# The joined score step of a fused attention and SwiGLU kernel: query groups stored one behind the other, and its exponential issued in two parts

## The chip, the cores and the metric

The kernel runs on one core of one Trainium2 chip. The metric is the device time of one execution in microseconds, smaller is better. The engines are named as in the profile: PE (matrix unit; PEld its weight loads), DVE (vector), ACT (scalar, with the exponentials), POOL (GpSimd) and SP (which here only issues DMAs).

## The reference

The attention has 8 batches of 8 heads, 576 positions and 64 values per head. Its result goes, row by row, through an RMS norm and a SwiGLU block.

```python
scores = scale * np.matmul(q, k.transpose(0, 1, 3, 2))          # B=8 H=8 S=576 D=64
cum = np.cumsum(np.maximum(s, 0.0), axis=-1)
bias = -(cum[:, :, :, None] - cum[:, :, None, :])
scores = np.where(causal, -1000000000.0, scores + np.minimum(bias, 0.0))
attn = softmax(scores)                                          # written out in the original
attn_out = np.matmul(attn, v)
x = attn_out.transpose(0, 2, 1, 3).reshape(B * S, H * D)        # 4608 x 512
xn = x / np.sqrt(np.mean(x * x, -1, keepdims=True) + 1e-6) * rms_g
g = xn @ w_gate                                                 # 512 -> 1536
out = (g * sigmoid(g) * (xn @ w_val)) @ w_out                   # 1536 -> 512
```

## The kernel before, in words

**The outer loop.** The 4608 tokens are worked off in nine chunks of 512 by `ffn(c)`. A chunk has twelve blocks of a gate product (L946) and a value product (L955), each of four matmuls into a bank `psF`; ACT takes the tanh (L949), DVE forms `U` (L958) and `Ht` (L951). Then `store` makes four output tiles of twelve matmuls each (L972), which ACT copies to `osb` (L976). Four `psF` banks are shared by all of these.

**What is threaded through it.** Between groups of matmuls `ffn` calls `step()`, a hand-written planner that counts slots. It puts a score step, a piece of attention-times-values (`av_step`, L437 and L443), a transpose or a DMA issue into the stream when its tables say that its inputs are due. The attention of batch b+1 and later is so computed beside the matmuls of earlier chunks. Each engine runs its instructions in the order in which they were written.

**How keys and queries lie.** For batches 3 to 7 (`MB = 3`), transposed keys and queries come from DMA transposes (L190, issued on SP) into `kqT`. The view `kqTx[d, parity, w, c, h, n]` has the chunk c of 128 positions, the pair of heads h, and position n. For queries (w = 1) of chunks 0 to 3 the 128 positions lie in the order (r p): position 4p + r stands at 32r + p. The 64 positions of the tail, chunk 4, lie in natural order. The two heads of a pair are on partitions 0 to 63 and 64 to 127, so that one matmul of 64 rows is issued for each (`par` 0 and 1).

**The score step.** `s_run(b, kb)` does one key chunk `kb` for all eight heads of such a batch. It takes four banks: one `psF`, one `psT`, and the two halves of `psS`; a bank holds two heads of 256 columns each (`j * 256`). For kb = 0, 1, 2 a head's 256 columns are the queries of chunks kb and kb+1. For kb = 3, the joined step (`join`), they are the 128 queries of chunk 3 against key chunk 3, the 64 tail queries against key chunk 3, and the 64 tail queries against key chunk 4. There is one joined step in each of the batches 3 to 7, five in all. In the kernel before, the three groups are interleaved in the bank: for each r the bank holds 32 columns of the first group, 16 of the second and 16 of the third. The tail is read with a step of four positions to fit.

**After the scores.** `exp_q` holds the four exponentials, one for each bank, and `step()` issues one per slot on ACT. Each one reads the bank with the (r p) order turned and writes `E` in natural order (bf16). After the second of a pair, POOL zeroes what lies above the diagonal (`mask`, L384): two selects in a joined step, one otherwise. `av_step` reads `E` as weights on PE some slots later.

Of the kernel before, what the change touches and what calls it, by code (L numbers as in the profile page):

```python
# [12 lines left out]
AF = mybir.ActivationFunctionType  # L13
# [13 lines left out]
def kernel(  # L27
# [12 lines left out]
    nc = tc.nc  # L40
# [41 lines left out]
    kqTx = kqT.rearrange("d a w (c h n) -> d a w c h n", c=NSC, h=HP)  # L82
# [26 lines left out]
    def psF():  # L109
        return pp.tile([128, DM], FP32, name="psF", tag="F", bufs=4)  # L110
# [4 lines left out]
    def psS():  # L115
        return pp.tile([128, 2, 512], FP32, name="psS", tag="S", bufs=1)
# [10 lines left out]
    def psT32():  # L127
        return pp.tile([128, 512], FP32, name="psT32", tag="T", bufs=1)
# [114 lines left out]
    def take_slot(key, reads):  # L243
        sl = ecount[0] % NE
        ecount[0] += 1
        eslot[key] = sl
        eread[sl] = reads
        return sl
# [90 lines left out]
    def s_run(b, kb):  # L339


        p, join = b % 2, kb == 3
        N = 192 if join else 256
        fb, tt, ps = psF(), psT32(), psS()
        banks = {1: (fb, tt), 0: (ps[:, 0, :], ps[:, 1, :])}
        es = {g: take_slot((b, kb, g), 3 if join else 2) for g in (1, 0)}
        if join:
            eslot.update({(b, 4, g): es[g] for g in es})

        def keys(rs, c, hp):  # L350
            return kqTx[rs, p, 0, c, hp, :] if b >= KB else kqTn[rs, p, 0, hp, c * 128:c * 128 + 128]

        for g in (1, 0):
            for j in (0, 1):
                hp = 2 * g + j
                parts = [(kb, kqTx[:, p, 1, kb:kb + 2, hp, :], 0, 256)]
                if join:
                    tail = kqTx[:, p, 1, 4, hp, 0:64].rearrange("d (p r) -> d r p", r=4)
                    parts = [(3, kqTx[:, p, 1, 3, hp, :].rearrange("d (r p) -> d r p", r=4), 0, 32),
                             (3, tail, 32, 16), (4, tail, 48, 16)]  # L360
                for i, (c, qT, o, n) in enumerate(parts):
                    for par in (0, 1):
                        rs = slice(par * 64, par * 64 + 64)
                        to = banks[g][par][:, j * 256:j * 256 + 256]
                        if join:
                            to = to.rearrange("k (r p) -> k r p", r=4)[:, :, o:o + n]
                        nc.tensor.matmul(to, lhsT=keys(rs, c, hp), rhs=qT[rs],  # L367
                                         start=(j == 0 and i == 0), stop=(j == 1 and i == len(parts) - 1))


        def exps(g, par):
            to = E[:, es[g], 2 * par:2 * par + 2, :]
            src = banks[g][par]
            if join:
                to = to.rearrange("k j (p r) -> k j p r", r=4)
                src = src.rearrange("k (j r p) -> k j p r", j=2, r=4)
            else:
                to = to.rearrange("k j (a p r) -> k (j a) p r", a=2, r=4)
                src = src.rearrange("k (j r p) -> k j p r", j=4, r=4)
            nc.scalar.activation(out=to, in_=src, func=AF.Exp, scale=0.125)  # L380

        def mask(g, c, q0, nq):
            Ev = E[:, es[g], :, q0:q0 + nq]
            nc.gpsimd.affine_select(  # L384
                out=Ev, in_=Ev, pattern=[[0, 4], [1, nq]], compare_op=ALU.is_ge, fill=0.0, base=0,
                channel_multiplier=-1)
            done["S", b, c, g] = slot[0]

        def part(g, par):
            exps(g, par)  # L390
            if g:
                last[("RA", "RT")[par]] = slot[0]
            if par:
                after(MLAG, lambda: mask(g, kb, 0, 128))
                if join:
                    after(MLAG, lambda: mask(g, 4, 192, 64))

        last["RA"] = last["RT"] = 10 ** 6
        exp_q.extend((join, lambda a=(g, par): part(*a)) for g in (1, 0) for par in (0, 1))
# [145 lines left out]
    def after(n, f):  # L545
        delayed.append((slot[0] + n, f))
# [158 lines left out]
    def do_s(key, pair=None, masked=False):  # L705
        b, kb, g = key
        last["S"] = done["R", b, kb] = slot[0]
        if b >= MB:
            last["run"] = done["R", b, 4] = slot[0]
            return s_run(b, kb)  # L710
        second = s_step(b, kb, g, pair, masked)
        done["S", b, kb, g] = slot[0]
        if kb == 4:
            done["S", b, 4, 1] = slot[0]
        return second
# [350 lines left out]
    with tc.manual_schedule():  # L1066
# [7 lines left out]
        for w in (0, 1):  # L1074
# [8 lines left out]
            out=mneg.rearrange("p (j n) -> p j n", j=2), in_=mneg.rearrange("p (j n) -> p j n", j=2),  # L1083
# [361 lines left out]
```

## Time and profile before

| | us |
|---|---|
| median of three runs (355.47 to 356.57) | 355.63 |
| the profiled execution | 355.58 |
| its span, first to last instruction | 354.1 |
| PE busy in the span | 340.6 (96%) |
| DVE, ACT, POOL busy | 276.9, 213.4, 204.5 |
| PE's granted clock, mean | 0.999 |

The profiled execution is 1.5 us longer than its span and 0.05 us below the median. A row of the timeline gives a start, a duration, the engine, the source line and what it writes and reads; where equal instructions follow each other they are one row with a count, whose duration runs from the first start to the last end. Matmuls overlap: their durations hold the way through the array, so that the distance of two starts, not the duration, says how long PE was taken.

### The profile page before, as it was taken

The page shows a single profiled execution, that of the slowest core. Times are in us where ns is not written, and L with a number is a line of the kernel's source. Part 1 is how long each engine was busy: PE and PEld are TensorE (multiplying, and loading weights), DVE is VectorE, ACT ScalarE, POOL GpSimd, SP SyncE. Part 2 cuts the span into 40 slices and gives each one's busy share as a digit, 9 for nine tenths or more (in the row PEclk, how much of TensorE's full clock was granted, in tenths as well). Part 3 has the DMA queues.
Part 4 walks back from the last instruction along what each step waited for, and adds up shares of the span by engine and source line. Part 5 has one row for each costly group of instructions (what it writes and reads, how often), then busy time and mean ns, then how long its engine had stood idle before and what let it go on. Part 6 is the DMA issues. An engine that isn't in the chain of part 4 may idle for free.

```text
span 354.1 us, 6889 instructions
## 1 busy us (share of the span) xinstructions
PE 340.6 (96%) x2374; PEld 165.3 (47%) x2419; DVE 276.9 (78%) x524; ACT 213.4 (60%) x471; POOL 204.5 (58%) x337
## 2 busy tenths in 40 slices
PE   5989999999999999999999999999999999999995
PEld 2445444544444444444554454444544554444443
DVE  6697989598967887798889887988798659836840
ACT  3988885878786546855677557654565445224321
POOL 6969754456769986687597987597745310000000
PEclk9999999999999999999999999999999999999999
DMA  7999999999969998999899999495510121020002
GB/s 220 142 213 270 180 175 259 181 211 181 98 123 177 146 179 118 233 141 202 143 170 105 117 131 185 46 113 90 143 29 17 57 94 23 0 91 30 0 34 93
DMA packets 130528, 45.68 MB, mean 129 GB/s; under 512 B 110548, under 2 KB 125656, under 8 KB 130488
## 3 DMA queue, kind: packets, MB, share of 16 engines
q0 software_dynamic: 67056, 13.70, 50.5%
q1 hardware_dynamic: 53792, 24.20, 33.3%
q10 hardware_dynamic: 9640, 7.29, 8.2%
q8 instruction: 20, 0.33, 0.4%
q14 instruction: 20, 0.16, 0.2%
HBM read 37.90 MB, written 9.44 MB: 134 GB/s over the span
## 4 chain that ended last, share of the span: by engine, by line
PE 77%; DVE 8%; POOL 4%; issue 4%; DMA 3%; ACT 2%; SPq 0%; DVEq 0%; POOLq 0%; ACTq 0%
PE psF L972 25%; PE psF L955 21%; PE psF L946 20%; DVE U L958 2%; PE psAV L443 2%; DMA kq<-in_q_dram 2%; DMA kqT<-kqn 2%; PE psS L286 2%; DVE Ht L951 1%; PE psAV L437 1%; DVE x_sb L453 1%; PE psF L367 1%; POOL v_sb L409 1%; POOL v_sb L194 1%; PE psS L367 1%
## 5 line engine op out<-in xcount | busy, mean ns | idle before, releaser
L955 PE MATMUL psF<-xnT,wv_sb 128*128 128x512 bf16 x424 | 109.9, 379 | 0.4
L946 PE MATMUL psF<-xnT,wg_sb 128*128 128x512 bf16 x414 | 109.0, 379 | 1.3 <-ACT xnT L511 0.3
L949 ACT ACTIVATE T<-psF 128x512 f32<-128x512 f32 x108 | 64.6, 598 | 62.9 <-PE psF L946 58.8
L972 PE MATMUL psF<-wout_sb,Ht 128*128 128x512 bf16 (+2 forms) x428 | 98.9, 373 | 1.4 <-issue 0.8
L958 DVE SCALAR_TENSOR_TENSOR U<-T,psF 128x512 bf16<-128x512 f32 x108 | 73.7, 682 | 24.1 <-ACT T L949 23.9
L951 DVE TENSOR_TENSOR Ht<-U,psF 128x512 bf16<-128x512 bf16 x99 | 67.8, 685 | 6.9
L972 PEld LDWEIGHTS <-Ht 128*128 128x128 bf16 x444 | 40.1, 98 | 43.5 <-issue 1.4
L955 PEld LDWEIGHTS <-wv_sb 128*128 128x128 bf16 x432 | 39.6, 98 | 44.5 <-issue 2.9
L946 PEld LDWEIGHTS <-wg_sb 128*128 128x128 bf16 x432 | 39.4, 98 | 42.9 <-issue 2.4
L976 ACT ACTIVATE osb<-psF 128x512 f32<-128x512 f32 (+2 forms) x37 | 21.7, 587 | 58.4 <-PE psF L972 50.8
L384 POOL TENSOR_SCALAR_AFFINE_SELECT E<-E 128x512 bf16<-128x512 bf16 (+1 forms) x50 | 34.8, 704 | 28.5 <-ACT E L380 18.7
L194 POOL DMA_DIRECT2D v_sb<-in_v_dram x40 | 35.3, 885 | 0.2 <-issue 0.2
L484 DVE SCALAR_TENSOR_TENSOR xs_sb<-x_sb,al_all,g_row 128x512 bf16<-128x512 bf16 (+1 forms) x36 | 29.6, 823 | 4.1 <-POOL al_all L477 3.9
L474 POOL TENSOR_SCALAR al_all<-ss_all 128x1 f32<-128x1 f32 (+2 forms) x39 | 11.5, 295 | 35.9 <-ACT xs_sb L461 27.9
L310 ACT ACTIVATE E<-psS,biasK 128x256 bf16<-128x256 f32 (+3 forms) x88 | 29.2, 426 | 2.6 <-PE psS L286 2.6
L453 DVE TENSOR_TENSOR x_sb<-psAV,rZ 128x256 bf16<-128x256 f32 (+1 forms) x66 | 28.0, 424 | 2.3
L522 DVE TENSOR_TENSOR acc<-acc,mag 128x1280 bf16<-128x1280 bf16 x32 | 27.3, 873 | 0.2
L477 POOL TENSOR_TENSOR al_all<-al_all,mhalf 128x1 f32<-128x1 f32 (+2 forms) x39 | 25.2, 645 | 3.2
L443 PEld LDWEIGHTS <-E 128*128 128x128 bf16 x320 | 21.7, 97 | 10.5 <-POOL E L384 0.7
L461 ACT ACTIVATE xs_sb<-x_sb 128x512 bf16<-128x512 bf16 (+1 forms) x37 | 23.3, 629 | 4.6 <-DVE x_sb L453 4.0
L409 POOL TENSOR_TENSOR v_sb<-v_sb,vwx 128x512 bf16<-128x512 bf16 x25 | 25.9, 1037 | 0.1
L443 PE MATMUL psAV<-v_sb,E 128*128 128x65 bf16 x264 | 23.8, 193 | 0.1
(136 smaller groups left out, 379.8 us busy)
## 6 DMA issues: line engine op xcount, KB each, us to landing
out_dram<-osb SPq DMA_DIRECT2D x35, 256.0 KB, 2.7
kq<-in_q_dram ACTq DMA_DIRECT2D x5, 1024.0 KB, 7.5
v_sb<-in_v_dram POOLq DMA_DIRECT2D x32, 128.0 KB, 4.9
kqn<-in_k_dram POOLq DMA_DIRECT2D x20, 128.0 KB, 5.1
kq<-in_k_dram SPq DMA_DIRECT2D x4, 512.0 KB, 5.8
kq<-in_q_dram SPq DMA_DIRECT2D x4, 512.0 KB, 7.5
wout_sb<-in_moe_w_out_dram POOLq DMA_DIRECT2D x2, 768.0 KB, 10.5
kq<-in_q_dram POOLq DMA_DIRECT2D x1, 1024.0 KB, 11.0
```

The source lines that it names most:

```text
L194: nc.gpsimd.dma_start(out=v_sb[0:n, b % 2, c, :, 0:64], in_=v[b, :, c * 128:c * 128 + n, :].rearrange("h p d -> p h d"))
L384: nc.gpsimd.affine_select(out=Ev, in_=Ev, pattern=[[0, 4], [1, nq]], compare_op=ALU.is_ge, fill=0.0, base=0, channel_multiplier=-1)
L409: nc.gpsimd.tensor_tensor(out=v_sb[:, b % 2, c, :, 0:64], in0=v_sb[:, b % 2, c, :, 0:64], in1=vwx[:, c, i:i + H].unsqueeze(2).to_broadcast ...
L443: nc.tensor.matmul(o, lhsT=d, rhs=v_sb[:, p, qb, h, :], start=(j == 0 and qb == 0), stop=(j == 3))
L453: nc.vector.tensor_tensor(out=xo[:, g * 256:(g + 1) * 256].rearrange("p (h d) -> p h d", h=4), in0=pv[R, :, 0:64], in1=rZ[R].unsqueeze(2). ...
L484: nc.vector.scalar_tensor_tensor(out=xs_sb[R, (b * NSC + qb) % NX, :], in0=x_sb[R, (b * NSC + qb) % NX, :], scalar=al_all[R, col:col + 1], ...
L946: nc.tensor.matmul(Gp, lhsT=wg_sb[:, cc, fs], rhs=xnT[:, cc, x0:x0 + DM], start=(cc == 0), stop=(cc == CC - 1))
L949: nc.scalar.activation(out=T, in_=Gp, func=AF.Tanh, scale=0.5)
L951: nc.vector.tensor_tensor(out=Ht[:, fb - 1, :], in0=pend[0], in1=pend[1], op=ALU.mult)
L955: nc.tensor.matmul(Vp, lhsT=wv_sb[:, cc, fs], rhs=xnT[:, cc, x0:x0 + DM], start=(cc == 0), stop=(cc == CC - 1))
L958: nc.vector.scalar_tensor_tensor(out=U, in0=T, scalar=1.0, in1=Gp, op0=ALU.add, op1=ALU.mult)
L972: nc.tensor.matmul(Op[:, p0:p1], lhsT=Ht[:, fb, tb * 128:(tb + 1) * 128], rhs=wout_sb[:, fb, p0:p1], start=(fb == 0), stop=(fb == FB - 1))
```

## The change

In the joined step the three groups of a head stand one behind the other in the bank: columns 0 to 127 the queries of chunk 3, in the (r p) order in which they are read, 128 to 191 the tail against key chunk 3, 192 to 255 the tail against key chunk 4, both in natural order. No operand of these matmuls is read or written with steps any more. As the two halves of a head's columns now need different reorderings, each exponential of a joined step is issued as two: one over columns 128 to 255 without reordering, one over 0 to 127 with the (r p) order turned. The steps for kb = 0, 1, 2 are as they were.

```diff
                 if join:
-                    tail = kqTx[:, p, 1, 4, hp, 0:64].rearrange("d (p r) -> d r p", r=4)
-                    parts = [(3, kqTx[:, p, 1, 3, hp, :].rearrange("d (r p) -> d r p", r=4), 0, 32),
-                             (3, tail, 32, 16), (4, tail, 48, 16)]
+                    tail = kqTx[:, p, 1, 4, hp, 0:64]
+                    parts = [(3, kqTx[:, p, 1, 3, hp, :], 0, 128), (3, tail, 128, 64), (4, tail, 192, 64)]
                 for i, (c, qT, o, n) in enumerate(parts):
                     for par in (0, 1):
                         rs = slice(par * 64, par * 64 + 64)
-                        to = banks[g][par][:, j * 256:j * 256 + 256]
-                        if join:
-                            to = to.rearrange("k (r p) -> k r p", r=4)[:, :, o:o + n]
+                        to = banks[g][par][:, j * 256 + o:j * 256 + o + n]
                         nc.tensor.matmul(to, lhsT=keys(rs, c, hp), rhs=qT[rs],
...
             to = E[:, es[g], 2 * par:2 * par + 2, :]
-            src = banks[g][par]
+            src = banks[g][par].rearrange("k (j n) -> k j n", j=2)
             if join:
-                to = to.rearrange("k j (p r) -> k j p r", r=4)
-                src = src.rearrange("k (j r p) -> k j p r", j=2, r=4)
+
+                nc.scalar.activation(out=to[:, :, 128:256], in_=src[:, :, 128:256], func=AF.Exp, scale=0.125)
+                to = to[:, :, 0:128].rearrange("k j (p r) -> k j p r", r=4)
+                src = src[:, :, 0:128].rearrange("k j (r p) -> k j p r", r=4)
             else:
```

PE's instructions at the first joined step, before. A row gives the line, the instruction, what it writes and reads, and the shape written; L972 is the output product around it, `psF` and `psT_2023` are the step's first two banks.

```order
L972 MATMUL psF<-wout_sb,Ht 128x512
L367 LDWEIGHTS kqT
L367 MATMUL psF<-kqT 128x4x32
L367 LDWEIGHTS kqT
L367 MATMUL psT_2023<-kqT 128x4x32
L367 LDWEIGHTS kqT
L367 MATMUL psF<-kqT 128x4x16
L367 LDWEIGHTS kqT
L367 MATMUL psT_2023<-kqT 128x4x16
L367 LDWEIGHTS kqT
L367 MATMUL psF<-kqT 128x4x16
```

The same place in the changed kernel, whose lines are numbered a few lower.

```order
L971 MATMUL psF<-wout_sb,Ht 128x512
L364 LDWEIGHTS kqT
L364 MATMUL psF<-kqT 128x128
L364 LDWEIGHTS kqT
L364 MATMUL psT_2023<-kqT 128x128
L364 LDWEIGHTS kqT
L364 MATMUL psF<-kqT 128x64
L364 LDWEIGHTS kqT
L364 MATMUL psT_2023<-kqT 128x64
L364 LDWEIGHTS kqT
L364 MATMUL psF<-kqT 128x64
```

Number, order and sizes of PE's instructions are the same; only the shape of what is written, and of what is read for the tail, is different.

ACT's instructions behind the same step, before: the four exponentials (L380) stand between the copies of the output tiles (L976), a sum of squares (L461) and a cast (L162).

```order
L976 ACTIVATE osb<-psF 128x512
L380 ACTIVATE E<-psF 128x512
L461 ACTIVATE xs_sb,ss_all<-x_sb 128x512
L380 ACTIVATE E<-psT_2023 128x512
L380 ACTIVATE E<-psS 128x512
L976 ACTIVATE osb<-psF 128x512
L380 ACTIVATE E<-psS 128x512
L162 ACTIVATE kqn<-kq_75 128x2x4x64
```

And in the changed kernel, with L373 the new first part and L379 the second.

```order
L975 ACTIVATE osb<-psF 128x512
L373 ACTIVATE E<-psF 128x2x128
L379 ACTIVATE E<-psF 128x2x128
L460 ACTIVATE xs_sb,ss_all<-x_sb 128x512
L373 ACTIVATE E<-psT_2023 128x2x128
L379 ACTIVATE E<-psT_2023 128x2x128
L373 ACTIVATE E<-psS 128x2x128
L379 ACTIVATE E<-psS 128x2x128
L975 ACTIVATE osb<-psF 128x512
L373 ACTIVATE E<-psS 128x2x128
L379 ACTIVATE E<-psS 128x2x128
L162 ACTIVATE kqn<-kq_75 128x2x4x64
```

Each exponential became two at the same place; nothing else moved on ACT, and DVE, POOL and SP have the same instructions in the same order.

More of the change, by code (lines that the diff above doesn't have):

```diff
@@ L372, in exps @@
             to = E[:, es[g], 2 * par:2 * par + 2, :]
-            src = banks[g][par]
+            src = banks[g][par].rearrange("k (j n) -> k j n", j=2)
             if join:
-                to = to.rearrange("k j (p r) -> k j p r", r=4)
-                src = src.rearrange("k (j r p) -> k j p r", j=2, r=4)
+                nc.scalar.activation(out=to[:, :, 128:256], in_=src[:, :, 128:256], func=AF.Exp, scale=0.125)
+                to = to[:, :, 0:128].rearrange("k j (p r) -> k j p r", r=4)
+                src = src[:, :, 0:128].rearrange("k j (r p) -> k j p r", r=4)
             else:
                 to = to.rearrange("k j (a p r) -> k (j a) p r", a=2, r=4)
-                src = src.rearrange("k (j r p) -> k j p r", j=4, r=4)
+                src = banks[g][par].rearrange("k (j r p) -> k j p r", j=4, r=4)
             nc.scalar.activation(out=to, in_=src, func=AF.Exp, scale=0.125)
```

## The prediction

> **What bounds the kernel now.** I read the page first.
>
> ```profile
> span 354.1 us, 6889 instructions
> PE 340.6 (96%) x2374; PEld 165.3 (47%) x2419; DVE 276.9 (78%) x524; ACT 213.4 (60%) x471; POOL 204.5 (58%) x337
> PE 77%; DVE 8%; POOL 4%; issue 4%; DMA 3%; ACT 2%; SPq 0%; DVEq 0%; POOLq 0%; ACTq 0%
> ```
>
> PE is busy for 96% of the span and holds 77% of the chain that ended last; ACT holds 2% of it. So time taken from PE counts nearly in full, and time added to ACT counts only where it delays something that PE needs. The list of waits shows what PE waits for around score steps.
>
> ```profile
> PE psF L972 <- issue: 0.8, 5, 0.2
> PEld L443 <- POOL E L384: 0.7, 2, 0.4
> PEld L367 <- DMA kqT<-kqn: 0.3, 1, 0.3
> ```
>
> The columns are total us, times, longest. The first row has exactly five waits, as many as there are joined steps. A wait for `issue` is one that the profile puts down to nothing: something inside PE. The timeline of PE shows the first joined step between matmuls of the output product.
>
> ```profile
> 131.54 0.23 PE L367 MATMUL psF<-kqT 64*128 64x128 bf16 x1
> 131.54 0.23 PE L367 MATMUL psT<-kqT 64*128 64x128 bf16 x1
> 131.60 0.22 PE L367 MATMUL psF<-kqT 64*128 64x64 bf16 x1
> ...
> 131.64 0.23 PE L367 MATMUL psF<-kqT 64*128 64x64 bf16 x1
> ...
> 131.70 0.23 PE L367 MATMUL psF<-kqT 64*128 64x128 bf16 x1
> ...
> 131.87 0.53 PE L367 MATMUL psS<-kqT 64*128 64x128 bf16 x12
> 132.56 0.81 PE L972 MATMUL psF<-wout_sb,Ht 128*128 128x512 bf16 x3 [0.16 <-issue]
> ```
>
> The two matmuls of a pair (`par` 0 and 1) start together, so I count pairs. From the first start to the next L972 PE is taken for 132.56 - 131.54 = 1.02 us: twelve pairs, 4 x (128 + 64 + 64) = 1024 columns. Two other blocks give a price for columns that lie in one row: the unjoined step, and the score step of 64 wide matmuls in an early batch.
>
> ```profile
> 140.69 0.28 PE L367 MATMUL psF<-kqT 64*128 64x256 bf16 x1
> ...
> 140.92 0.38 PE L367 MATMUL psS<-kqT 64*128 64x256 bf16 x4
> 141.23 0.82 PE L972 MATMUL psF<-wout_sb,Ht 128*128 128x512 bf16 x3
> ```
> ```profile
> 62.02 0.29 PE L286 MATMUL psS<-kqT 64*128 64x64 bf16 x8
> 62.24 0.82 PE L972 MATMUL psF<-wout_sb,Ht 128*128 128x512 bf16 x3
> ```
> ```profile
> L367 PE MATMUL psF<-kqT 64*128 64x64 bf16 x20 | 2.4, 224 | 0.1
> ...
> L286 PE MATMUL psS<-kqT 64*128 64x64 bf16 x24 | 0.9, 192 | 0.0
> ```
>
> The unjoined step has the same 1024 columns in four pairs and takes 141.23 - 140.69 = 0.54 us, about half of the joined one. Four pairs of 64 columns take 62.24 - 62.02 = 0.22 us. The last two rows say the same of a single matmul: 64 columns take 192 ns where they lie in a row and 224 ns in the joined step.
>
> **Part one: the matmuls.** Between the two blocks without steps there are 768 columns and 0.32 us: 0.417 ns a column. What one more pair costs beside its columns is read from the 64 wide block: its eight starts lie within 0.29 - 0.19 = 0.10 us (whole row less the last duration), three distances of 0.033 us, of which 64 columns are 0.027; that leaves at most 0.006. The joined step written and read in a row is therefore the unjoined one with eight more pairs: 0.54 us at least, 0.54 + 8 x 0.006 = 0.59 at most; I take 0.56. The gain is 1.02 - 0.56 = **0.46 us a joined step** (0.43 to 0.48).
>
> A second way through the same rows agrees. Two heads' worth of starts, 131.54 to 131.87, is 0.33 us, where 512 columns with four pairs of overhead more would be 0.22 to 0.25: four heads lose some 0.16 to 0.2. The rest is behind the last start. It is at 131.87 + 0.53 - 0.23 = 132.17 and the next L972 follows 0.39 later; in the 64 wide block the last start is at 62.12 and L972 follows 0.12 later. So 0.27 us, the 0.16 of `issue` among it, is a backlog: PE takes these matmuls in faster than it finishes them.
>
> The other four joined steps look alike (the five waits of 0.16 us; the third step's rows stand here), except that the second waits for a transfer in its middle.
>
> ```profile
> 204.18 0.23 PE L367 MATMUL psF<-kqT 64*128 64x128 bf16 x1
> ...
> 205.20 0.59 PE L972 MATMUL psF<-wout_sb,Ht 128*128 128x512 bf16 x2 [0.16 <-issue]
> ```
> ```profile
> 167.86 0.21 PE L367 MATMUL psF<-kqT 64*128 64x64 bf16 x1
> ...
> 168.18 0.22 PE L367 MATMUL psF<-kqT 64*128 64x64 bf16 x1
> ...
> 169.08 0.59 PE L972 MATMUL psF<-wout_sb,Ht 128*128 128x512 bf16 x2 [0.16 <-issue]
> ```
>
> The second step spends 168.18 - 167.86 = 0.32 us where the first spends 0.04, waiting for the tail's transposes; its backlog at the end is the same. Five times 0.46 is **2.3 us**. If the transfer's landing were fixed in time, what the first step gains would be lost in this wait, and 4 x 0.46 = 1.84 us would be left. I count all five, because the chain leads from that transfer back to work that itself follows PE.
>
> ```profile
> 158.31 0.59 DVE U L958
> 158.90 0.67 DVE xs_sb L484
> ...
> 161.09 1.21 SPq L190
> ...
> 162.40 5.73 DMA kqT<-kqn
> ```
>
> The transpose was issued behind POOL's and DVE's work of the same slots, and `U` is made from PE's products; all of it comes earlier when PE does.
>
> The Trainium skill has a rule on such patterns. Its page "PSUM — Partial Sum Buffer", section Specifications, says of the 8-byte lines of PSUM that any access pattern that is not contiguous slows matmuls significantly; it gives no figure. By that rule, the trace agrees: 1.02 against 0.54 us for equal columns.
>
> **Part two: the exponentials.** Twenty exponentials of 512 columns become forty of 256. The rows around the first joined step, and earlier ones of other widths:
>
> ```profile
> 133.41 0.60 ACT L976 ACTIVATE osb<-psF 128x512 f32<-128x512 f32 x1 [3.65 <-PE psF L972]
> ...
> 135.83 0.59 ACT L380 ACTIVATE E<-psS 128x512 bf16<-128x512 f32 x1
> 136.31 0.60 ACT L976 ACTIVATE osb<-psF 128x512 f32<-128x512 f32 x1
> 136.79 0.61 ACT L380 ACTIVATE E<-psS 128x512 bf16<-128x512 f32 x1
> ...
> 138.83 0.60 ACT L976 ACTIVATE osb<-psF 128x512 f32<-128x512 f32 x1 [0.92 <-PE psF L972]
> ```
> ```profile
> 10.17 0.71 ACT L151 ACTIVATE kqn<-kq 128x256 bf16<-128x256 f32 x2
> ...
> 18.17 0.87 ACT L326 ACTIVATE E<-psS 128x384 bf16<-128x384 f32 x2
> ```
> ```profile
> L151 ACT ACTIVATE kqn<-kq 128x256 bf16<-128x256 f32 x4 | 1.4, 408 | 0.8 <-DMA kq<-in_q_dram 0.8
> ...
> L326 ACT ACTIVATE E<-psS 128x384 bf16<-128x384 f32 x2 | 0.9, 488 | 0.0
> ```
>
> One of 512 columns keeps ACT for 136.31 - 135.83 = 0.48 us. Two of 384 take 0.87, so one keeps it for 0.87 - 0.488 = 0.38; 128 columns are 0.10, which makes 256 columns 0.28. Two casts of 256 take 0.71, so 0.71 - 0.408 = 0.30 each. Two halves then take 0.56 to 0.60 instead of 0.48: 0.08 to 0.12 more an exponential, 0.3 to 0.5 us a joined step, 1.6 to 2.4 us of ACT in all.
>
> This is beside the path. ACT waited 3.65 us for PE ahead of these exponentials and 0.92 us behind them. The `osb` copy at 136.31 comes up to 0.36 us later, but its bank is one of four, and PE has no wait for ACT's copies in its list. Behind ACT stand the masks on POOL, and behind those PE's reading of `E`:
>
> ```profile
> 137.55 2.98 POOL L384 TENSOR_SCALAR_AFFINE_SELECT E<-E 128x512 bf16<-128x512 bf16 x4
> ```
> ```profile
> 142.11 0.19 PE L437 MATMUL psAV<-v_sb,E 128*128 128x65 bf16 x1
> ```
>
> The masks end at 140.53 and the next read of `E` is at 142.11, 1.58 us later; a delay of 0.5 us fits. PE waited for a mask only twice in the kernel (0.7 us). If that cover were gone, up to 0.5 us a joined step would show. I take nothing.
>
> The Trainium skill's page "ScalarE: Activation LUTs", section What ACT_TABLE_LOAD costs, speaks against the change: an ACTIVATE has a fixed part of 186 ns, of which some 93 ns overlap with its neighbour, so twenty more would be an estimated 1.9 us of ACT. By that rule, the rows agree (1.6 to 2.4 us); were ACT the bound, the change would lose about this much.
>
> **The sum.** 355.58 us of the profiled execution less 2.3 is 353.3. That execution is 0.05 us below the median of the runs, so 353.3 stands for the median too.
>
> **The rivals.**
>
> *Half of it.* PE gains, but the transfer at 168.18 keeps its time, or DVE's chain holds the next gate blocks where they are, since DVE is at 78%. Against it speaks that joined steps lie among output products, where DVE has no `U` or `Ht` to make. With half of 2.3 us gone: 354.4.
>
> *No gain.* The joined block may be slow not for its steps but for its mix: 24 key loads, widths of 128 and 64 in turn, three groups in a bank. All that stays. Against it: the 64 wide block also loads new keys for each matmul and puts four groups into a bank, at 0.033 us a pair. The mix of widths is in no other block. PE then stays at 1.02 us a step and ACT's extra is hidden: 355.6. The Trainium skill's page "Advanced Engine Details and Errata", section Memory Cachelines, can be read for this: two hits on a 16-byte line of SBUF are enough for full speed, and two fp32 values in a row suffice in PSUM. The tail's step of four bf16 values hits each line twice, and runs of 16 and 32 columns are whole lines; by that reading the old pattern cost nothing. The 0.54 us of the unjoined step speaks against it.
>
> *Slower.* Later masks hold up POOL. POOL issues the loads of keys and values, and the transposes on SP come behind them; PE already waited once for such a transpose (the 0.32 us above). This decides once a mask's delay, 0.3 to 0.5 us, reaches the issue of a transfer on which a score step waits, and PE's gain is under that. With 0.4 us lost behind each of four joined steps and the gain only a tenth: 355.6 + 1.6 - 0.2 = 357.0. Against it: POOL is at 58%, and such a wait appears once in 354 us.
>
> **How the numbers follow.** The forecast, 353.3, has a chance of 0.70, half of it 0.10, no gain 0.11, slower 0.09. About 0.3% of 355.63, 1.07 us, is what a measurement of this kernel can tell from no change; the line to faster is at 354.56. The forecast and over half of the second case lie below it: faster 0.76. No gain and the rest: same 0.15. Slower 0.09. The range begins at 352.6: the most a step may gain, 5 x 0.48 = 2.4, the wait of 0.28 at 167.86 gone with it, and the runs' own spread of some 0.3 below. It ends at 355.3, which takes in half of the gain and a part of the case without any.
>
> **What would show it.** In the changed kernel's timeline the joined block should take 0.54 to 0.59 us from its first start to the next L971, with its matmuls of 64 columns near 192 ns and without the five waits of 0.16. ACT's busy time should grow while its waits for PE shrink, and PE's waits for masks stay below 1 us. A block that stays near 1 us makes the prediction wrong at its first step; a block of 0.56 us with an unchanged span means that the gain went into a wait, and the list of PE's waits should name it.

## The result, and the profile after

| | before | changed | |
|---|---|---|---|
| median of 21 runs each, us | 355.99 | 355.01 | ratio 0.9967, interval 0.9957 to 0.9977 |
| profiled execution, us | 355.58 | 354.37 | |
| its span, us | 354.1 | 352.9 | |

The ratio is that of the means, 355.03 and 356.20 us, with its 95% interval. By it the changed kernel is faster by 0.33% (0.23 to 0.43%), 1.17 us; the medians are 0.98 us apart. That is a change clear of the noise, but only about half of the 2.3 us that were forecast. The page of the changed kernel:

```profile
span 352.9 us, 6909 instructions
PE 339.1 (96%) x2374; PEld 164.0 (46%) x2419; DVE 276.7 (78%) x524; ACT 214.4 (61%) x491; POOL 203.6 (58%) x337
PE 77%; DVE 8%; DMA 4%; POOL 4%; issue 4%; ACT 2%; SPq 1%; DVEq 0%; POOLq 0%; ACTq 0%
```

PE is busy for 1.5 us less, ACT for 1.0 us more; PE's share of the chain is the same. The list of PE's waits, the same three rows as before:

```profile
PE psF L971 <- issue: 0.8, 5, 0.2
PEld L442 <- POOL E L383: 0.7, 2, 0.4
PEld L364 <- DMA kqT<-kqn: 0.3, 1, 0.3
```

The five waits of 0.16 us for `issue` are all still there. The timeline of PE at the first joined step shows both what was gained and what seems to have stayed:

```profile
131.44 0.23 PE L364 MATMUL psF<-kqT 64*128 64x128 bf16 x1
...
131.51 0.19 PE L364 MATMUL psF<-kqT 64*128 64x64 bf16 x1
...
131.53 0.19 PE L364 MATMUL psF<-kqT 64*128 64x64 bf16 x1
...
131.56 0.22 PE L364 MATMUL psF<-kqT 64*128 64x128 bf16 x1
...
131.68 0.39 PE L364 MATMUL psS<-kqT 64*128 64x128 bf16 x12
132.23 0.81 PE L971 MATMUL psF<-wout_sb,Ht 128*128 128x512 bf16 x3 [0.16 <-issue]
```

A head's three pairs now start within 131.56 - 131.44 = 0.12 us (0.16 before), and a matmul of 64 columns takes 0.19 (0.21 to 0.24 before). But by the recorded matmuls PE is taken from 131.44 to 132.23, 0.79 us, where 0.56 was forecast. The last row holds the answer. `store` issues four L971 matmuls up to the next `step()`, and three are recorded. The weight loads are all there. Their rows of the changed kernel, and below of the one before:

```profile
131.44 0.51 PEld L364 LDWEIGHTS <-kqT 64*128 64x128 bf16 x24 [0.42 <-issue]
132.00 0.55 PEld L971 LDWEIGHTS <-Ht 128*128 128x128 bf16 x4
```
```profile
131.53 0.69 PEld L367 LDWEIGHTS <-kqT 64*128 64x128 bf16 x24 [0.42 <-issue]
132.33 0.55 PEld L972 LDWEIGHTS <-Ht 128*128 128x128 bf16 x4
```

Four loads, the first of them at 132.00 and at 132.33. If the matmul that belongs to the first load ran right behind it and is only missing from the trace, the joined step took 132.33 - 131.54 = 0.79 us before, and 132.00 - 131.44 = 0.56 us after: 0.23 us a step, 1.15 us in five steps, which is near what the runs show. The other reading is that the gap is real, that PE has a backlog behind 24 short matmuls, and that the change did not touch it.

### The profile page after: what moved, and what is told of

Its sections match the earlier page's. It is cut to its first block, busy times and chain, and to the rows that moved or that the text cites. A ratio compares the mean times of both kernels' runs of the same rounds, so it can differ in the third digit from the quotient of the medians.

```text
span 352.9 us, 6909 instructions
## 1 busy us (share of the span) xinstructions
PE 339.1 (96%) x2374; PEld 164.0 (46%) x2419; DVE 276.7 (78%) x524; ACT 214.4 (61%) x491; POOL 203.6 (58%) x337
## 4 chain that ended last, share of the span: by engine, by line
PE 77%; DVE 8%; DMA 4%; POOL 4%; issue 4%; ACT 2%; SPq 1%; DVEq 0%; POOLq 0%; ACTq 0%
PE psF L971 25%; PE psF L954 21%; PE psF L945 21%; DMA kq<-in_q_dram 2%; DVE U L957 2%; PE psAV L442 2%; DMA kqT<-kqn 2%; PE psS L286 2%; DVE Ht L950 2%; PE psAV L436 1%; DVE x_sb L452 1%; PE psF L364 1%; POOL v_sb L408 1%; DVE xs_sb L483 1%; PE psS L364 1%
## 5 line engine op out<-in xcount | busy, mean ns | idle before, releaser
L971 PE MATMUL psF<-wout_sb,Ht 128*128 128x512 bf16 (+2 forms) x428 | 98.9, 373 | 1.4 <-issue 0.8
L971 PEld LDWEIGHTS <-Ht 128*128 128x128 bf16 x444 | 40.1, 98 | 43.3 <-issue 1.4
```

Source lines behind the costliest of these rows:

```text
L971: nc.tensor.matmul(Op[:, p0:p1], lhsT=Ht[:, fb, tb * 128:(tb + 1) * 128], rhs=wout_sb[:, fb, p0:p1], start=(fb == 0), stop=(fb == FB - 1))
```

## The experiments

Theory A is the missing record, theory B the real backlog, theory C that the exponentials' halves took back what PE gained. Theories R and W, further down, say that the reads or the writes in steps were the cost.

**The exponentials in parts, nothing else.** The scores stay as before.

```diff
             if join:
                 to = to.rearrange("k j (p r) -> k j p r", r=4)
                 src = src.rearrange("k (j r p) -> k j p r", j=2, r=4)
+                nc.scalar.activation(out=to[:, 0], in_=src[:, 0], func=AF.Exp, scale=0.125)
+                to, src = to[:, 1], src[:, 1]
```

> The kernel before, its scores still interleaved, but each of the twenty joined exponentials issued as two of 256 columns (one for each head). Theory A (the first output matmul behind a joined step is missing from the trace, so that PE gained only 0.23 us a step, and the exponentials' halves cost nothing): no change, within 0.4 us of before (ratio 0.999 to 1.001), ACT busy about 1 us more. Theory B (PE's backlog behind the joined step is real and stayed): the same, no change. Theory C (PE gained 2.3 us and the halves took 1.1 us of it back): 1.1 us slower, ratio 1.003.

Measured: 1.0009 (0.9996 to 1.0023) against before. The interval ends at 0.23%, some 0.8 us, so theory C has at most a part of its 1.1 us. The timeline of PE at the first joined step of this run says more than its time. PE's instructions are those of the kernel before:

```profile
131.94 0.23 PE L367 MATMUL psF<-kqT 64*128 64x128 bf16 x1
...
132.28 0.53 PE L367 MATMUL psS<-kqT 64*128 64x128 bf16 x12
132.74 1.04 PE L974 MATMUL psF<-wout_sb,Ht 128*128 128x512 bf16 x4
133.61 0.19 PE L439 MATMUL psAV<-v_sb,E 128*128 128x65 bf16 x1
```

In this trace all four output matmuls are recorded. The first starts 132.74 - 131.94 = 0.80 us behind the step's first, without a wait for `issue`; the row of five waits is gone from the list. What follows the four, attention times values, says the same without any record in question. It starts 133.61 - 131.94 = 1.67 us behind the step's first matmul here, and 133.21 - 131.54 = 1.67 in the kernel before, where three are recorded. So the gap in the trace of before was a missing record and not time. The same stretch in the changed kernel is 132.88 - 131.44 = 1.44 us, 0.23 less. First the row of before, then that of the changed kernel:

```profile
133.21 0.19 PE L437 MATMUL psAV<-v_sb,E 128*128 128x65 bf16 x1
```
```profile
132.88 0.19 PE L436 MATMUL psAV<-v_sb,E 128*128 128x65 bf16 x1
```

The page of this run shows how far the records are complete: it has as many matmuls as weight loads, 2419, where the pages of before and of the changed kernel have 2374 matmuls for 2419 loads.

```profile
PE 343.2 (97%) x2419; PEld 165.1 (47%) x2419; DVE 276.7 (78%) x524; ACT 214.7 (61%) x491; POOL 205.3 (58%) x337
```

So 45 matmuls are missing there, five of them behind the joined steps. PE's busy time can be compared only between profiles that miss as many, as those of before and of the changed kernel do.

**The changed kernel with one exponential a bank.**

```diff
-            src = banks[g][par].rearrange("k (j n) -> k j n", j=2)
-            if join:
-                nc.scalar.activation(out=to[:, :, 128:256], in_=src[:, :, 128:256], func=AF.Exp, scale=0.125)
-                to = to[:, :, 0:128].rearrange("k j (p r) -> k j p r", r=4)
-                src = src[:, :, 0:128].rearrange("k j (r p) -> k j p r", r=4)
-            else:
-                to = to.rearrange("k j (a p r) -> k (j a) p r", a=2, r=4)
-                src = banks[g][par].rearrange("k (j r p) -> k j p r", j=4, r=4)
+            to = to.rearrange("k j (a p r) -> k (j a) p r", a=2, r=4)
+            src = banks[g][par].rearrange("k (j r p) -> k j p r", j=4, r=4)
```

> The changed kernel with one exponential of 512 columns a bank, as in the unjoined steps; the 64 tail queries of a joined step then come out in a wrong order, and nothing else is different. Theory A: as the changed kernel, 1.0 to 1.2 us below before (ratio 0.9967), joined blocks as in the changed kernel. Theory B: the same. Theory C: the whole gain appears, 2.3 us below before (ratio 0.9935).

Measured: 0.9970 (0.9954 to 0.9987), the changed kernel's own ratio; theory C asked for 0.9935 and falls. Here, too, the record is there, with PE's joined step as in the changed kernel:

```profile
132.68 0.23 PE L364 MATMUL psF<-kqT 64*128 64x128 bf16 x1
...
132.91 0.39 PE L364 MATMUL psS<-kqT 64*128 64x128 bf16 x12
133.24 1.04 PE L964 MATMUL psF<-wout_sb,Ht 128*128 128x512 bf16 x4
```

133.24 - 132.68 = 0.56 us, the forecast block.

**Each joined step's matmuls twice.** The same edit in the changed kernel and in the one before.

```diff
-        for g in (1, 0):
+        for g in (1, 0) * (2 if join else 1):
             for j in (0, 1):
```

> The changed kernel with the 24 matmuls of each joined step issued twice in a row (the second set overwrites the first with the same values). Theory A: a second set costs its columns alone, 12 pairs at 440 + 26 ns, 0.46 us a step, 2.3 us in all: 1.2 us above before (ratio 1.0033). Theory B: it also doubles the backlog, 0.46 + 0.23 = 0.69 us a step, 3.4 us in all: 2.3 us above before (ratio 1.0065).

> The kernel before with the 24 matmuls of each joined step issued twice in a row. Theory A: 0.63 + 0.06 = 0.69 us a step, 3.4 us in all (ratio 1.0097). Theory B: with a backlog of 0.23 us more a set, 0.92 us a step, 4.6 us in all (ratio 1.013). Under both the last start to the next recorded output matmul stays near 0.39 us; under theory A it stays because one record is missing, and there are three or seven output matmuls recorded up to the next other work instead of four or eight.

Measured: the changed kernel doubled 1.0033 (1.0020 to 1.0045), the one before doubled 1.0099 (1.0085 to 1.0114, from four runs). Theory A had said 1.0033 and 1.0097, theory B 1.0065 and 1.013; both of B's lie outside. This rests on no single record. By the ratios 24 matmuls more cost some 0.47 us a step in one pattern and 0.71 in the other, near the 0.46 and 0.69 us from the first set's start to the second's, and nothing behind it. First the changed kernel doubled, then the one before:

```profile
132.06 0.23 PE L364 MATMUL psF<-kqT 64*128 64x128 bf16 x1
...
132.52 0.22 PE L364 MATMUL psF<-kqT 64*128 64x128 bf16 x1
```
```profile
132.54 0.23 PE L367 MATMUL psF<-kqT 64*128 64x128 bf16 x1
...
133.23 0.24 PE L367 MATMUL psF<-kqT 64*128 64x128 bf16 x1
```

The other forecast, on what the trace would show, was wrong: no record is missing in either run, so the last start to the next output matmul is 0.12 (changed, doubled) and 0.17 us (before, doubled), not 0.39.

**Which steps cost.** The first run reads the tail in a row and still writes in steps; the second reads in steps and writes in a row. In both, each joined exponential is issued in three parts, which are left out of the edits here.

```diff
-                    tail = kqTx[:, p, 1, 4, hp, 0:64].rearrange("d (p r) -> d r p", r=4)
+                    tail = kqTx[:, p, 1, 4, hp, 0:64].rearrange("d (r p) -> d r p", r=4)
...
```
```diff
-                    tail = kqTx[:, p, 1, 4, hp, 0:64]
+                    tail = kqTx[:, p, 1, 4, hp, 0:64].rearrange("d (p r) -> d r p", r=4)
                     parts = [(3, kqTx[:, p, 1, 3, hp, :], 0, 128), (3, tail, 128, 64), (4, tail, 192, 64)]
...
+                        if join and o:
+                            to = to.rearrange("k (r p) -> k r p", r=4)
...
```

> The kernel before with one thing undone: the tail's queries are read in a row (natural order), while the scores are still written in steps (4 x 32 and 4 x 16 columns); each joined exponential is issued in three parts to put the columns in order. What is open is which of the two patterns cost the 0.23 us of PE a step. Theory R (the reads of the tail in steps of four did it): first to last start of a joined step near 0.44 us as in the changed kernel, total near the changed kernel's (ratio 0.997). Theory W (the writes in steps did it): 0.63 us as before, ratio 1.000.

> The changed kernel with the tail's queries read in steps of four again, and written in a row; each joined exponential in three parts. Theory R: first to last start near 0.63 us, ratio 1.000. Theory W: 0.44 us, ratio 0.997. If each pattern does a part, both this run and the one with reads in a row lie between.

Measured: 0.9981 (0.9962 to 0.9999) and 1.0007 (0.9993 to 1.0020). The first leaves out theory W's 1.000 only just; the second leaves out W's 0.997. The groups of PE's instructions are sharper than the times. First the run that reads in a row, then the one that writes in a row:

```profile
L367 PE MATMUL psF<-kqT 64*128 64x64 bf16 x20 | 1.8, 190 | 0.0
```
```profile
L366 PE MATMUL psF<-kqT 64*128 64x64 bf16 x20 | 2.4, 224 | 0.3 <-DMA kqT<-kqn 0.2
```

And their timelines at the first joined step, in the same order:

```profile
132.38 0.23 PE L367 MATMUL psF<-kqT 64*128 64x128 bf16 x1
...
132.62 0.39 PE L367 MATMUL psS<-kqT 64*128 64x128 bf16 x12
```
```profile
132.02 0.23 PE L366 MATMUL psF<-kqT 64*128 64x128 bf16 x1
...
132.37 0.52 PE L366 MATMUL psS<-kqT 64*128 64x128 bf16 x12
```

With the last matmul's 0.19 and 0.24 us taken off, the last start is 132.62 + 0.39 - 0.19 - 132.38 = 0.44 us behind the first where the tail is read in a row, and 132.37 + 0.52 - 0.24 - 132.02 = 0.63 where it is read in steps. The third to fifth joined steps give the same 0.44 and 0.63. Theory R holds and W falls: the reads in steps of four cost all of it, and writing 4 x 32 or 4 x 16 columns into a bank adds nothing that is seen here.

**How much ACT may do.** Both parts of each joined exponential are issued twice.

```diff
                 nc.scalar.activation(out=to[:, :, 128:256], in_=src[:, :, 128:256], func=AF.Exp, scale=0.125)
+                nc.scalar.activation(out=to[:, :, 128:256], in_=src[:, :, 128:256], func=AF.Exp, scale=0.125)
                 to = to[:, :, 0:128].rearrange("k j (p r) -> k j p r", r=4)
                 src = src[:, :, 0:128].rearrange("k j (r p) -> k j p r", r=4)
+                nc.scalar.activation(out=to, in_=src, func=AF.Exp, scale=0.125)
```

> The changed kernel with both parts of each joined exponential issued twice (the same values again), to find how much cover ACT has: 4 x 0.52 = 2.1 us more of ACT behind each joined step, 10.4 us in all. Theory A (all of ACT's part is hidden, with a cover of about 1.6 us up to the next read of E behind the first step): up to 0.5 us a step show, 2.6 us in all, ratio against before 0.997 to 1.004. Theory D (the cover is wider than 2.1 us): as the changed kernel, 0.997. Theory C (what ACT does more shows): 10 us slower, ratio 1.026.

Measured: 1.0004 (0.9986 to 1.0021), some 0.37% above the changed kernel's ratio: 1.3 us of the 10.4 added show, inside what theory A allowed, and not what D or C said. They do not come where I put them: the two waits for masks in PE's list are as before. In the two profiles PE falls back behind the changed kernel at two places above all. The first joined step starts 0.49 us later than there (131.93 against 131.44), the first gate product behind it 0.96 later. It waits for a transpose of `xnT`. First the changed kernel, then this run:

```profile
138.65 1.18 SPq L494 DMA_TRANSPOSE xnT<-xs_sb  x1
...
142.02 1.03 PE L945 MATMUL psF<-xnT,wg_sb 128*128 128x512 bf16 x4
```
```profile
137.99 1.12 DVE L484 SCALAR_TENSOR_TENSOR xs_sb<-x_sb,al_all,g_row 128x512 bf16<-128x512 bf16 x1 [0.46 <-POOL al_all L477]
138.81 0.59 ACT L976 ACTIVATE osb<-psF 128x512 f32<-128x512 f32 x1
139.43 0.33 SPq L977 DMA_DIRECT2D out_dram<-osb  x1
139.85 1.19 SPq L495 DMA_TRANSPOSE xnT<-xs_sb  x1
142.98 1.02 PE L946 MATMUL psF<-xnT,wg_sb 128*128 128x512 bf16 x4 [0.31 <-DMA xnT<-xs_sb]
```

`xs_sb` is ready at 139.11 here. But on SP the store of an output tile stands ahead of its transpose, and that store waits for ACT's copy (`osb`), which stands behind the doubled exponentials and ends at 139.40. So 0.47 us of PE's time hang on a copy, not on a mask. The other place is a wait for a transpose of `kqT`, at an unjoined step between the first two joined ones:

```profile
PE psF L364 <- DMA kqT<-kqn: 1.5, 1, 1.5
```
```profile
154.66 3.49 SPq L190 DMA_TRANSPOSE kqT<-kqn  x2
```

These two transposes begin to be issued 0.96 us later than in the changed kernel (153.70), no more than PE itself is late by then. Neither a late cast nor a late mask is seen in that. What is longer is the issuing of the two, 3.49 us against 2.58. Whether ACT's extra work caused this was not tested.

**The tail's pairs last.** The joined step does its four pairs of 128 columns first.

```diff
-        for g in (1, 0):
-            for j in (0, 1):
...
-                for i, (c, qT, o, n) in enumerate(parts):
+        order = [(g, j, i) for g in (1, 0) for j in (0, 1) for i in range(1)]
+        if join:
+            order += [(g, j, i) for g in (1, 0) for j in (0, 1) for i in (1, 2)]
+        for g, j, i in order:
...
```

> The changed kernel with the order of the joined step's pairs turned: first the four of 128 columns, then the eight of the tail, so that the second joined step, which waits 0.33 us in its middle for the tail's transposes, has 0.17 us more to do ahead of that wait. If the transposes' landing is fixed: 0.17 us less, at most 0.2 us below the changed kernel (ratio against before 0.996 to 0.997). If something else ends the wait, no change from the changed kernel.

Measured: 0.9964 (0.9952 to 0.9975), not to be told from the changed kernel's 0.9967. In its profile the second joined step still waits for the tail's transposes:

```profile
168.29 0.19 PE L366 MATMUL psF<-kqT 64*128 64x64 bf16 x1
...
168.75 0.20 PE L366 MATMUL psF<-kqT 64*128 64x64 bf16 x1 [0.26 <-DMA kqT<-kqn]
```

168.75 - 168.29 = 0.46 us, against 0.35 in the changed kernel's profile. How long this wait is differs by more than the 0.17 us that the order can save: in four profiles in which a joined step takes 0.44 us from first to last start, the second one takes 0.55 (tail read in a row, written in steps), 0.77 (changed kernel), 0.87 (this run) and 1.09 (one exponential a bank). Nothing that was tried beats the changed kernel clearly.

## Why the prediction was wrong

**What failed is the size of the block before.** The step was: "From the first start to the next L972 PE is taken for 132.56 - 131.54 = 1.02 us". The next recorded L972 was the second one; the first ran at 132.33. The block was 0.79 us, so the gain of a step was 0.23 and not 0.46, and the sum 1.15 and not 2.3 us. The whole difference follows from that one misread row. The "second way through the same rows" was none: it used the same missing record, and took "0.27 us, the 0.16 of `issue` among it" for a backlog. Its first half, 0.16 to 0.2 us lost between the starts, was right (0.19 in the runs). The five waits for `issue`, put down to "something inside PE", were the same missing records.

The trace of before could have said so. The prediction's rows behind the other two blocks also count three L972 matmuls, but those rows are cut off by the end of the stretch shown; the whole row of the unjoined step has four:

```profile
141.23 1.04 PE L972 MATMUL psF<-wout_sb,Ht 128*128 128x512 bf16 x4
```

The whole row behind the joined step has three, where the code has four and PEld's row has four loads. The page that the prediction opens with shows it for the whole kernel, in x2374 for PE and x2419 for PEld. That the record was missing five times out of five, at the same place, made it look like a mechanism.

**What PE takes after the change was right.** 0.54 to 0.59 us was forecast from the two blocks in a row; 0.56 was measured. So was the place. Where the five joined steps start in the two profiles shows that the gain arose in them and was kept to the end:

| | before, us | changed, us | changed ahead by |
|---|---|---|---|
| first joined step starts | 131.54 | 131.44 | 0.10 |
| second | 167.80 | 167.47 | 0.33 |
| third | 204.18 | 203.69 | 0.49 |
| fourth | 240.70 | 239.97 | 0.73 |
| fifth | 276.82 | 275.85 | 0.97 |
| end of the span | 354.1 | 352.9 | 1.2 |

Four steps gave 0.23 or 0.24 us each. The second gave 0.16, as its wait for the tail's transposes was longer; the prediction had counted all five alike. From the first joined step on that is 1.1 us in these two profiles, and by the ratio the runs give 1.17.

**The cause was right only in part.** The prediction put the cost down to operands that do not lie in a row, read or written, and quoted the page "PSUM — Partial Sum Buffer" of the Trainium skill for it, that any access pattern in PSUM that is not contiguous slows matmuls significantly. The runs say otherwise: with writes in runs of 16 and 32 columns the step took the same 0.44 us as without. That the trace agreed with that rule, 1.02 against 0.54 us, was a misreading: the block was 0.79 us, and what it took beyond the 0.56 of the changed kernel came from the reads. The rival "no gain" was right about these writes and wrong about the reads. It took the Trainium skill's page "Advanced Engine Details and Errata", section Memory Cachelines, to say that two hits on a line of SBUF are enough. The tail's step of four bf16 values makes two, and that read cost 0.19 us a step between the starts and some 0.04 behind. Why such a read is slower was not tested.

**ACT's part was hidden, as forecast, and smaller.** The forecast was 0.56 to 0.60 us for two halves. The timeline of ACT in the changed kernel:

```profile
135.25 0.36 ACT L373 ACTIVATE E<-psT 128x256 bf16<-128x256 f32 x1
135.52 0.37 ACT L379 ACTIVATE E<-psT 128x256 bf16<-128x256 f32 x1
135.78 0.38 ACT L373 ACTIVATE E<-psS 128x256 bf16<-128x256 f32 x1
136.04 0.39 ACT L379 ACTIVATE E<-psS 128x256 bf16<-128x256 f32 x1
136.31 0.62 ACT L975 ACTIVATE osb<-psF 128x512 f32<-128x512 f32 x1
```

The starts are 0.26 us apart, 0.52 for two halves against 0.48 for a whole one: 0.04 us more, where 0.08 to 0.12 were forecast. All twenty make 0.8 us by this, and ACT's busy time grew by 1.0, not by the 1.6 to 2.4 of the forecast. That it was hidden fits the two kernels in which only the exponentials were exchanged: 1.0009 against before, whose interval allows at most 0.8 us, and 0.9970 beside the changed kernel's 0.9967. The masks of the first joined step still end well ahead of PE's next read of `E`:

```profile
137.44 2.98 POOL L383 TENSOR_SCALAR_AFFINE_SELECT E<-E 128x512 bf16<-128x512 bf16 x4
```
```profile
141.78 0.19 PE L436 MATMUL psAV<-v_sb,E 128*128 128x65 bf16 x1
```

They end at 140.42, 1.36 us ahead of the read, against 1.58 before. With 2.1 us more of ACT a step, part of it showed, but at a transpose and not at the masks.

**The rivals.** "Half of it" named 354.4 us, near the measured gain, but that is luck: nothing took half of the gain back, it was only half as large. "No gain" and "slower" did not come. The slower rival looked for trouble in the transposes on SP, and there the doubled exponentials showed, though by way of ACT's copies and their stores and not of POOL's masks.

## What to carry to other kernels

Before a gap between two recorded matmuls is priced, count the records around it against the code and against the weight loads, and compare the counts of PE and PEld on the page; a matmul that is not in the trace looks just like a wait for nothing. A price for a block is safer when it comes from doing the block twice than from its edge. Here an operand that PE streams (the 64 tail queries) cost twice its columns' time when it was read in steps of four bf16 values, and it was cheaper to read it in a row and let ACT, which had the time, put the order right in one more instruction.

## What the runs showed of the hardware that was not expected

A strided write of PE into a bank, in runs of 16 or 32 fp32 columns, added nothing here: 0.44 us from first to last start of a joined step with it and without it. A strided read by PE of 64 bf16 values, in steps of four, cost about as much again as the read itself: a set of matmuls takes PE for 0.69 us instead of 0.46, which is 0.23 / 8 = 0.029 for each of its eight pairs of 64 columns, where 64 columns in a row are 0.027. And the profiler left out the same number of matmuls, 45 of 2419, in six of the profiles (before, changed, and the last four experiments), the first one behind each of the five joined steps among them, and none in the other four, two of which have the PE instructions of before and of the changed kernel.
